# Routing of a mixture of experts inside attention: new segments, capped steps, masks and counts made otherwise

## The chip, the cores and the metric

One Trainium2 chip, one of its cores. The metric is the device time of one execution in microseconds. Below, PE is TensorE, DVE VectorE, ACT ScalarE, POOL GpSimd, and SP the engine that issues most transfers.

## The reference, cut to what matters

Local attention with a few global columns (4 batches, 8 heads, 768 positions, head size 64) makes x, 3072 rows of 512. Then each row goes to two of eight experts:

```python
logits = x @ w_gate
noisy = logits + log1p(exp(x @ w_noise)) * noise
top2 = argpartition(-noisy, 2)[:, :2]; top2_w = softmax of the two
for e in range(8):                       # F = 1024, D = 512
    h = maximum(x[mask] @ w1[e], 0)
    out[mask] += top2_w * (h @ w2[e])
```

## The kernel before

The 3072 rows are 24 blocks of 128 tokens (six to a batch). **Attention** is a loop of 48 rounds, numbered 0 to 47, two to a block; a round takes four heads. Its work is software-pipelined: `score(n+2)` (DVE adds the bias and takes the maximum, ACT exponentiates), `trans` (PE), `product(n+4)` (PE, into the two banks that `score` has just read), `norm(n-4)` (DVE), `attend(n-2)` (PE). Block g is gated in rounds 2g+4 and 2g+5: `gate_t` (transposes, and a copy by POOL that is stored to `xd`), `gate_l` and `gate_s` (logits, made for two blocks at once, and alone for the last block of a segment of odd length).

**Routing** (`route`) is a generator for each segment of consecutive blocks. Its steps: softplus of the noise logits by a polynomial; the two best experts of a token (MAX8 and index, a block each); weights (`weigh`); one-hot counts summed over tokens by PE (lines 530 to 534), which with `carry`, the count of all segments before, give every token its slot in its expert's list; then for each block and choice a mask of the slot's low seven bits (`mask`, line 559, into `wall`, 5 buffers) and a product of value and band (`marks`, line 587), which PE multiplies (line 612) and DVE adds to `tab` (line 615). So segments must pass the counts in order. Steps are dealt out to rounds: `tick(place)` issues one step at each of seven places of a round (0 to 3 in `score`, 4 to 6 in `norm`), `finish()` up to 5 (3 for segments 0 and 1) at its end. A step that yields True goes on at place 4 of the next round, one that yields LAST at place 6, one that yields 2 at `finish`. Segment CLOSE = 2 goes first.

When CLOSE is done, expert 0's first 512 slots are complete enough to use: four `gather`s (POOL's indirect transfers, one a round), then four `whole_words` (16 copies by POOL), then `turn` (PE transposes, ACT and DVE) and **up(0)**: 96 matmuls of 512 columns, with 32 slots between them. The two last segments, `late` (index 3) and `last` (index 4), are advanced in these slots to step numbers that a table gives (`slots`); `split` makes expert 0's second weights. After up(0) DVE does the other six `split`s, the last `tab`, and `rank()`, which orders the experts by count; after it POOL gathers the tokens of expert 0's tail and of expert 1, and weights of ranked experts are fetched. The experts run to the end one after another.

```python
SEG = [(0, 6), (6, 12), (12, 17), (17, 21), (21, NT)]
gather(0, t, DUMP + z * P); yield LAST       # t = 0..3, after CLOSE's last tab
for t in range(TA): whole_words(0, t); yield
for x in pending: x.upto(99)                 # after up(0) and the splits
rank()
```

## Time and profile before

| what | value |
|---|---|
| median of 3 runs (range) | 710.76 us (708.8 to 712.78) |
| the profiled execution, its span | 717.22 us, 715.4 us |
| PE busy, weight loads | 690.2 us (96%), 617.7 us (86%) |
| DVE, ACT, POOL busy | 469.7 us (66%), 425.0 us (59%), 330.0 us (46%) |
| granted PE clock | 0.997 |

Busy time of PE has modelled ends, so a round's length is read from the starts of its matmuls. Attention's last round ends at about 161 us, up(0) runs from 165.77 to 192.42 us, `rank()` ends at about 202.5 us.

### The profile page before, as it was taken

The page shows a single profiled execution, that of the slowest core. Times are in us where ns is not written, and L with a number is a line of the kernel's source. Part 1 is how long each engine was busy: PE and PEld are TensorE (multiplying, and loading weights), DVE is VectorE, ACT ScalarE, POOL GpSimd, SP SyncE. Part 2 cuts the span into 40 slices and gives each one's busy share as a digit, 9 for nine tenths or more (in the row PEclk, how much of TensorE's full clock was granted, in tenths as well). Part 3 has the DMA queues.
Part 4 walks back from the last instruction along what each step waited for, and adds up shares of the span by engine and source line. Part 5 has one row for each costly group of instructions (what it writes and reads, how often), then busy time and mean ns, then how long its engine had stood idle before and what let it go on. Part 6 is the DMA issues. An engine that isn't in the chain of part 4 may idle for free.

```text
span 715.4 us, 16240 instructions
## 1 busy us (share of the span) xinstructions
PE 690.2 (96%) x5769; PEld 617.7 (86%) x5769; DVE 469.7 (66%) x1478; ACT 425.0 (59%) x909; POOL 330.0 (46%) x424
## 2 busy tenths in 40 slices
PE   6999999999999989999999999999999999999995
PEld 5888888877789879999989998999899899889984
DVE  6659898967957557736774686567576766666600
ACT  6888777763427477545854676476558556745510
POOL 3363626372078862074607461644465344642222
PEclk9999999999999999999999999999999999999998
DMA  9997678775086795156935681768459646943233
GB/s 246 317 288 229 205 235 278 229 272 216 0 219 152 130 205 153 16 94 154 184 83 112 169 210 49 135 162 176 76 127 196 128 117 159 204 74 89 31 45 47
DMA packets 129913, 111.10 MB, mean 155 GB/s; under 512 B 51578, under 2 KB 96762, under 8 KB 129824
## 3 DMA queue, kind: packets, MB, share of 16 engines
q1 hardware_dynamic: 118416, 83.84, 43.4%
q0 software_dynamic: 11264, 25.89, 19.8%
q8 instruction: 47, 0.77, 0.5%
q10 hardware_dynamic: 144, 0.26, 0.2%
q14 instruction: 42, 0.34, 0.2%
HBM read 71.07 MB, written 27.59 MB: 138 GB/s over the span
## 4 chain that ended last, share of the span: by engine, by line
PE 67%; DVE 10%; issue 8%; DMA 5%; ACT 4%; POOL 4%; SPq 0%; POOLq 0%; ACTq 0%; DVEq 0%
PE bank L1410 24%; PE av L1148 20%; PE av L878 5%; PE sc L827 4%; PE at L857 4%; PE av L1171 4%; DMA xt<-xg 2%; PE at L1111 2%; DVE xl L196 1%; PE sc L1111 1%; DMA xg<-xd,ids 1%; POOL out_dram L1124 1%; DVE ns L841 1%; PE m L397 1%; ACT xg L277 1%
## 5 line engine op out<-in xcount | busy, mean ns | idle before, releaser
L1410 PE MATMUL bank<-xh,wall 128*128 128x384 f32 (+4 forms) x784 | 216.8, 343 | 3.9 <-ACT aside L1451 3.9
L1410 PEld LDWEIGHTS bank<-xh,wall 128*128 128x128 f32 x784 | 143.8, 188 | 8.3 <-ACT aside L1451 4.7
L1410 PE MATMUL bank<-xl,wall 128*128 128x384 f32 (+4 forms) x392 | 133.3, 340 | 0.0
L1148 PE MATMUL av<-w2h,hh 128*128 128x512 f32 x304 | 119.8, 394 | 2.0 <-ACT aside L1180 1.4
L1124 POOL DMA_INDIRECT out_dram<-y,ids x40 | 63.6, 1590 | 125.6 <-ACT y L1121 121.3
L1148 PE MATMUL av<-w2h,hl 128*128 128x512 f32 x304 | 119.1, 392 | 0.0
L1148 PE MATMUL av<-w2l,hh 128*128 128x512 f32 x304 | 119.0, 391 | 0.0
L196 DVE TENSOR_TENSOR wall<-raw,wall 128x512 fp32r<-128x512 f32 (+1 forms) x84 | 77.7, 931 | 56.0 <-ACT wall L195 55.9
L195 ACT ACTIVATE wall<-raw 128x512 fp32r<-128x512 f32 (+1 forms) x84 | 58.0, 698 | 45.7 <-POOL raw L1256 45.6
L1096 DVE SCALAR_TENSOR_TENSOR hl<-bank,hh 128x384 fp32r<-128x384 f32 (+4 forms) x84 | 47.2, 562 | 55.0 <-ACT hh L1092 52.7
L844 ACT ACTIVATE a<-ns,mx 128x168 f32<-128x168 f32 (+1 forms) x192 | 67.9, 423 | 20.1 <-DVE mx L841 19.4
L243 POOL DMA_INDIRECT xg<-xd,ids x53 | 56.2, 1060 | 45.4 <-DVE place L297 32.5
L1410 PEld LDWEIGHTS bank<-xl,wall 128*128 128x128 f32 x392 | 73.9, 188 | 2.8
L1148 PEld LDWEIGHTS av<-w2h,hl 128*128 128x128 f32 x304 | 57.1, 188 | 12.6
L1148 PEld LDWEIGHTS av<-w2h,hh 128*128 128x128 f32 x304 | 57.2, 188 | 11.6 <-ACT aside L1180 1.7
L1148 PEld LDWEIGHTS av<-w2l,hh 128*128 128x128 f32 x304 | 57.1, 188 | 9.3 <-DVE w2l L196 0.3
L841 DVE CUSTOM_DVE_ANT_0 ns<-sc,bias 128x168 f32<-128x168 f32 (+1 forms) x188 | 51.8, 320 | 19.1 <-PE sc L827 14.1
L1092 ACT ACTIVATE hh<-bank 128x384 fp32r<-128x384 f32 (+4 forms) x84 | 41.8, 498 | 37.5 <-DVE bank L1483 24.0
L1255 POOL TENSOR_TENSOR raw<-raw 128x256 f32<-128x256 f32 x28 | 22.1, 791 | 82.1 <-DVE wall L196 81.4
L235 POOL COPY xt<-y 128x256 uint16<-128x256 uint16 x96 | 35.2, 403 | 51.5 <-DVE y L894 51.5
L878 PE MATMUL av<-vs,at 128*64 128x65 f32 (+1 forms) x768 | 57.3, 224 | 0.0
L878 PEld LDWEIGHTS av<-vs,at 128*64 128x64 f32 (+1 forms) x768 | 50.9, 136 | 2.4 <-issue 2.0
(219 smaller groups left out, 1494.8 us busy)
## 6 DMA issues: line engine op xcount, KB each, us to landing
raw<-in_w SPq DMA_DIRECT2D x64, 256.0 KB
raw<-in_w SPq DMA_DIRECT2D x32, 512.0 KB
out_dram<-zero SPq DMA_DIRECT2D x14, 512.0 KB
vs<-in_v SPq DMA_DIRECT2D x24, 260.0 KB
xd<-xt SPq DMA_DIRECT2D x24, 256.0 KB
qbuf<-in_q SPq DMA_DIRECT2D x23, 256.0 KB
ks<-in_k SPq DMA_DIRECT2D x20, 272.0 KB
vp<-in_v SPq DMA_DIRECT2D x20, 195.0 KB
```

The lines of the kernel that those rows point to most:

```text
L195: nc.scalar.activation(hi, src, AF.Copy)
L196: eng.tensor_sub(lo, src, hi.bitcast(F32))
L235: nc.gpsimd.tensor_copy(to[:, :, c], frm[:, :, c])
L243: nc.gpsimd.indirect_dma_start(out=xg[e, t].bitcast(U16)[:m], out_offset=None, in_=xd[:n], in_offset=bass.IndirectOffsetOnAxis(ap=r, axis= ...
L841: nc.vector.tensor_tensor_reduce(out=ns[x][:, s, :w], in0=ps[:, s], in1=bias[:, u + x, s] if i else bias0[:, u + x, s], scale=-scale, scal ...
L844: nc.scalar.activation(A[n + x][:, s * w:(s + 1) * w], ns[x][:, s, :w], AF.Exp, bias=mx[x][:, s:s + 1], scale=-1.0)
L878: nc.tensor.matmul(ps[s * Q:(s + 1) * Q, h], a[r:z, part * P + q0:part * P + q0 + Q], t[r:z, c], start=k == 0 and (n == 1 or h == 0), stop ...
L1092: nc.scalar.activation(inner(e)[0][j][:, f, :src.shape[1]], src, AF.Relu)
L1096: nc.vector.scalar_tensor_tensor(lo, src, 0.0, hi.bitcast(F32), op0=OP.max, op1=OP.subtract)
L1124: ins = nc.gpsimd.indirect_dma_start(out=out, out_offset=bass.IndirectOffsetOnAxis(ap=r, axis=0), in_=y, in_offset=None, bounds_check=N + ...
L1148: nc.tensor.matmul(ps, x[j][:, f, cols], w[:, f], start=n == 0, stop=n == 3 * FC - 1)
L1410: nc.tensor.matmul(ps, wb[c % 2][u][:, 2 * a + k], x[v][:, 2 * b + k], start=start and n == 0, stop=stop and n == 5, skip_group_check=True)
```

## The change

Segments become 6, 4, 6, 4, 4 blocks, all even, so every block is gated in a pair; CLOSE ends at block 15 instead of 16, so it starts two rounds earlier, and the gathers of expert 0 draw on 16 blocks. Each round may issue at most 5, 5, 9 and 4 steps of segments 0 to 3, and 7 of segments 0 and 1 together. The counts are one matmul of all blocks by `upper` and w by `ones`, each shifted by one block. The two `marks` of a block are one operation of twice the size. Masks are kept in 12 buffers; those of segments 0, 1 and 3 are made by POOL, some rounds or slots ahead, those of CLOSE and of the last segment by DVE (before: 0, 1 and CLOSE by POOL, the others by DVE). Each segment has one group of matmuls at line 612 instead of groups of three blocks. The slots of up(0) are dealt anew.

```diff
--- before.py
+++ after.py
@@ -63,7 +63,7 @@
     windowed = 1 <= n_local <= NP + 1 and 0 <= n_global <= NG
     scale = 1.0 / math.sqrt(D)
     slopes = [2.0 ** (-8.0 * (h + 1) / H) for h in range(H)]
-    SEG = [(0, 6), (6, 12), (12, 17), (17, 21), (21, NT)]
+    SEG = [(0, 6), (6, 10), (10, 16), (16, 20), (20, NT)]
     CLOSE = 2
     SW = max(z - a for a, z in SEG)
 
@@ -524,14 +524,13 @@
         else:
             yield 2
         ps = lgp
-        pos = ps[:, E:(w + 1) * E].rearrange("p (t e) -> p t e", t=w)
-        tot = ps[:, :E]
-        for i in range(w):
-            nc.tensor.matmul(pos[:, i], upper, ohs[:, i], start=True, stop=i == 0)
-            for j in range(i):
-                nc.tensor.matmul(pos[:, i], ones, ohs[:, j], start=False, stop=j == i - 1)
-        for j in range(w):
-            nc.tensor.matmul(tot, ones, ohs[:, j], start=j == 0, stop=j == w - 1)
+        pos = ps[:, :w * E].rearrange("p (t e) -> p t e", t=w)
+        tot = ps[:, w * E:(w + 1) * E]
+        of = ohs.rearrange("p t e -> p (t e)")
+        nc.tensor.matmul(ps[:, :w * E], upper, of, start=True, stop=False, skip_group_check=True)
+        for d in range(1, w + 1):
+            nc.tensor.matmul(ps[:, d * E:(w + 1) * E], ones, of[:, :(w + 1 - d) * E], start=False, stop=d == w,
+                             skip_group_check=True)
         if r != CLOSE:
             yield from some(4)
         else:
@@ -554,10 +553,10 @@
         put_in = {}
 
         def mask(i):
-            m = wts.tile([P, 2, P], FR, name="m", bufs=5)
+            m = wts.tile([P, 2, P], FR, name="m", bufs=12)
             for j in range(2):
-                (nc.vector if r > CLOSE else nc.gpsimd).tensor_scalar(m[:, j], iota_p, row[:, i, j:j + 1], None,
-                                                                      op0=OP.is_equal)
+                (nc.vector if r in (CLOSE, len(SEG) - 1) else nc.gpsimd).tensor_scalar(m[:, j], iota_p, row[:, i, j:j + 1], None,
+                    op0=OP.is_equal)
             put_in[i] = m
 
         nc.vector.tensor_copy(si, sl)
@@ -565,10 +564,6 @@
         nc.vector.tensor_scalar(si, si, P - 1, None, op0=OP.bitwise_and)
         yield
         nc.vector.tensor_copy(row, si)
-        if r == CLOSE and not marking:
-            marking.append(r)
-            for i in range(w):
-                mask(i)
         yield
         nc.vector.tensor_sub(fs, sl, row)
         yield
@@ -576,41 +571,44 @@
         nc.vector.tensor_tensor(band, fs[:, :, :, None].to_broadcast(bs),
                                 first[:, None, None, :].to_broadcast(bs), op=OP.is_equal)
         yield
-        size = w if r == CLOSE else 3
+        size = w
         groups = [range(i, min(i + size, w)) for i in range(0, w, size)]
         def marks(i):
             b = gp.tile([P, Dm], F32, name="xg", bufs=7)
             c = b[:, :6 * E * TT].bitcast(FR).rearrange("p (j x t) -> p j x t", j=2, t=TT)
-            cs = [P, 3 * E, TT]
-            for j in range(2):
-                what = ev[:, i, j].rearrange("p x e -> p (x e)")[:, :, None]
-                nc.vector.tensor_tensor(c[:, j], what.to_broadcast(cs),
-                                        band[:, i, j][:, None, :].to_broadcast(cs), op=OP.mult)
+            cs = [P, 2, 3 * E, TT]
+            what = ev[:, i].rearrange("p j x e -> p j (x e)")[:, :, :, None]
+            nc.vector.tensor_tensor(c, what.to_broadcast(cs), band[:, i][:, :, None, :].to_broadcast(cs), op=OP.mult)
             put_in[i] = put_in[i], c
 
-        while r <= CLOSE and marking and marking != [r]:
-            yield True
-        if r not in marking:
-            marking.append(r)
+        if r <= CLOSE:
+            for i in range(w):
+                mask(i)
+                yield True if r < CLOSE and i % 2 else None
+            while marking:
+                yield True
+        elif r < len(SEG) - 1:
+            for i in range(w):
+                mask(i)
+            yield
+        marking.append(r)
         for x, gr in enumerate(groups):
-            if r <= CLOSE and not put_in:
-                for i in gr:
-                    mask(i)
             for i in gr:
-                if r > CLOSE:
-                    mask(i)
-                marks(i)
-                if r == CLOSE:
-                    yield 2 if i == w - 1 else True if i == 1 else None
+                if r <= CLOSE:
+                    marks(i)
+                    yield 2 if i == w - 1 else True if i % 2 else None
                 else:
-                    yield from (None, ) if r < CLOSE else (None, ) * 3
-            if r != CLOSE:
-                yield from (True, 2) if r < CLOSE else (None, ) * 3
+                    if i not in put_in:
+                        mask(i)
+                    marks(i)
+                    yield from (None, ) * 3
+            if r > CLOSE:
+                yield from (None, ) * 3
             ps = lgp[:, (SW + 1) * E:][:, :3 * E * TT]
             m = [(m[:, j], c[:, j]) for i in gr for m, c in [put_in.pop(i)] for j in range(2)]
             for k, (l, o) in enumerate(m):
                 nc.tensor.matmul(ps, l, o, start=k == 0, stop=k == len(m) - 1)
-            yield LAST if r == CLOSE else True
+            yield LAST if r <= CLOSE else True
             yield
             nc.vector.tensor_add(tab, tab, ps.rearrange("p (x e t) -> p x e t", x=3, e=E))
             yield
@@ -775,12 +773,21 @@
 
         END, WAIT = 7, 8
 
+        PACE = {0: 5, 1: 5, 2: 9, 3: 4, 'all': 7}
+        left = {}
+
         def begin():
+            left.update(PACE)
             for x, _ in active:
                 x.ready = {WAIT: 4, WAIT + 1: 6}.get(x.ready, 0)
 
+        def may(r):
+            return left[r] > 0 and (r >= CLOSE or left['all'] > 0)
+
         def go(y):
             x = y[0]
+            for r in (y[1], 'all') if y[1] < CLOSE else (y[1], ):
+                left[r] -= 1
             v = next(x, 0)
             if v == 0:
                 active.remove(y)
@@ -793,13 +800,13 @@
 
         def tick(place):
             for y in sorted(active, key=lambda y: y[1] != CLOSE):
-                if y[0].ready <= place:
+                if y[0].ready <= place and may(y[1]):
                     return go(y)
 
         def finish():
             for y in active[:]:
                 n = 5 if y[1] >= CLOSE else 3
-                while n and y in active and y[0].ready <= END:
+                while n and y in active and y[0].ready <= END and may(y[1]):
                     go(y)
                     n -= 1
 
@@ -1197,13 +1204,13 @@
         late, last = pending
         slots = {
             0: [(late, 24)], 1: [gate_t, (late, 27)], 2: [(late, 30)], 3: [gate_l, (late, 33)],
-            4: [(late, 36)], 5: [gate_s, (late, 39)], 6: [(late, 42)], 7: [(late, 45), (last, 2)],
-            8: [], 9: [(late, 48), (last, 5)], 10: [(last, 7)], 11: [(last, 8)],
-            12: [(late, 52), (last, 9)], 13: [(last, 12)], 14: [(last, 14)], 15: [(late, 54), (last, 16)],
-            16: [(last, 19)], 17: [(last, 21)], 18: [(last, 23)], 19: [(last, 26)],
-            20: [(last, 30)], 21: [(last, 33)], 22: [(late, 57), (last, 35)], 23: [(last, 37)],
-            24: [(last, 39)], 25: [(last, 42)], 26: [(late, 61)], 27: [(last, 45)],
-            28: [(last, 48)], 29: [(late, 99), split], 30: [split], 31: [(last, 52)],
+            4: [(late, 37)], 5: [gate_s, (late, 40)], 6: [(late, 43)], 7: [(late, 46), (last, 2)],
+            8: [(last, 4)], 9: [(late, 49), (last, 6)], 10: [(last, 8)], 11: [(last, 10)],
+            12: [(late, 52), (last, 12)], 13: [(last, 14)], 14: [(last, 16)], 15: [(late, 55), (last, 18)],
+            16: [(last, 20)], 17: [(last, 23)], 18: [(last, 25)], 19: [(last, 27)],
+            20: [(late, 57)], 21: [(last, 29)], 22: [(late, 99)], 23: [(last, 33)],
+            24: [(last, 36)], 25: [(last, 39)], 26: [(last, 42)], 27: [(last, 45)],
+            28: [(last, 48)], 29: [(last, 51), split], 30: [split, (last, 54)], 31: [(last, 55)],
         }
         slot, parts = [0], [0]
 
```

## Rows read from the trace of the kernel before

**Rows 1.** Windows view; four rounds a row, last up(0): window, length, busy (instructions), PEclk, DMA.
```profile
32.88:44.52 11.64, 11.64 (x250) 10.12 (x243) 6.95 (x44) 10.26 (x29) 6.08 (x8) 1.00 1.05 334
...
56.42:70.72 14.30, 13.70 (x280) 11.69 (x273) 13.10 (x89) 11.51 (x32) 5.39 (x15) 1.00 0.69 203
70.72:82.93 12.21, 12.21 (x256) 10.82 (x249) 10.36 (x63) 9.78 (x28) 8.84 (x18) 1.00 0.70 204
...
94.90:108.16 13.26, 13.17 (x279) 11.50 (x272) 12.13 (x87) 10.44 (x30) 3.06 (x9) 1.00 0.79 231
...
120.38:132.95 12.57, 12.25 (x212) 9.96 (x207) 11.69 (x86) 8.88 (x28) 4.47 (x11) 1.00 1.00 310
132.95:149.04 16.09, 15.28 (x284) 13.08 (x278) 13.29 (x78) 10.96 (x31) 10.75 (x20) 1.00 0.45 137
...
165.77:192.42 26.65, 26.39 (x147) 20.92 (x148) 23.36 (x124) 7.23 (x16) 0.28 (x1) 1.00 0.30 109
```
**Rows 2.** Timeline of TensorE: the counts of segment 0, and the start of up(0).
```profile
68.19 0.20 PE L530 MATMUL lg<-aside,upper 128*128 128x8 bf16 x2
...
68.88 0.31 PE L857 MATMUL at<-ident,a 128*128 128x128 f32 x1
...
163.61 1.47 PE L342 MATMUL sc<-ident,xg 128*128 128x128 f32 x8 [0.49 <-POOL xg L235]
...
165.77 0.50 PE L1111 MATMUL at<-wall,xh 128*128 128x512 f32 x1 [0.54 <-ACT wall L344]
```
**Rows 3.** Chain that ended last, 136 to 167 us: start us, us, what.
```profile
139.89 4.50 POOL wall L559 x7
...
150.64 0.40 issue
...
151.43 0.35 issue
```
**Rows 4.** Timeline of GpSimd at the end of attention.
```profile
155.22 1.03 POOL L243 DMA_INDIRECT xg<-xd,ids  x1
156.25 1.65 POOL L235 COPY xg<-xg 128x256 uint16<-128x256 uint16 x4
...
159.97 4.73 POOL L235 COPY xg<-xg 128x256 uint16<-128x256 uint16 x12
```
**Rows 5.** Timeline of VectorE: small routing operations, then the end of up(0) and after.
```profile
130.43 0.15 DVE L483 MAX8 aside<-aside 128x8 f32<-128x8 f32 x1
...
130.64 0.15 DVE L483 MAX8 aside<-aside 128x8 f32<-128x8 f32 x1
...
177.97 0.18 DVE L462 TENSOR_TENSOR aside<-aside 128x24 f32<-128x24 f32 x1
178.19 0.18 DVE L464 TENSOR_TENSOR aside<-aside 128x24 f32<-128x24 f32 x1
...
188.94 0.48 DVE L559 TENSOR_SCALAR wall<-iota_p,aside 128x128 fp32r<-128x128 f32 x2
189.33 0.57 DVE L587 TENSOR_TENSOR xg<-aside 128x168 fp32r<-128x168 f32 x2
189.82 0.69 DVE L1096 SCALAR_TENSOR_TENSOR hl<-at,hh 128x512 fp32r<-128x512 f32 x1
...
192.74 0.69 DVE L1096 SCALAR_TENSOR_TENSOR hl<-sc,hh 128x512 fp32r<-128x512 f32 x1
...
196.95 0.33 DVE L615 TENSOR_TENSOR tab<-tab,lg 128x168 f32<-128x168 f32 x1
```
**Rows 6.** Operations of lines 587, 559 and 307: count, duration min/median/max ns, first and last start.
```profile
L587 DVE TENSOR_TENSOR xg<-aside x48: 316/327/500, 75.5 to 191.1; 128x168 fp32r<-128x168 f32 x48
...
L559 POOL TENSOR_SCALAR wall<-iota_p,aside x34: 594/636/882, 74.9 to 143.8; 128x128 fp32r<-128x128 f32 x34
L559 DVE TENSOR_SCALAR wall<-iota_p,aside x14: 278/281/286, 173.0 to 190.6; 128x128 fp32r<-128x128 f32 x14
...
L307 DVE TENSOR_TENSOR xg<-perm,tab x2: 808/809/810, 199.2 to 200.5; 128x343 f32<-128x343 f32 x2
```

## The prediction

> **What bounds the kernel now.** I read the busy times first: PE is the engine that is nearly always occupied, so a change in routing can pay only where it takes work or waiting off PE's path. Second, the windows view, cut at the first `attend` matmul of every fourth round, tells where routing costs time. Four rounds without routing take 11.64 us, all of it PE [rows 1]; that is my floor. The reader is to see that length follows VectorE's load: 6.95 us of DVE at the floor, 10.36 in a window of 12.21 us, 12.13 in 13.26, 13.10 in 14.30, 13.29 in 16.09 [rows 1]. The reason is in the code: `product(n+4)` writes the banks that `score(n+2)` reads, and each of score's four operations has a routing step behind it in DVE's queue.
>
> Not all above the floor is waiting; some is PE's own routing work. The counts of a six-block segment, 27 matmuls, hold PE from 68.19 to 68.88 us [rows 2], 0.69 us or 0.0256 each. The 0.57 us over the floor in the window from 70.72, where DVE does not press, I take as one group of six matmuls of line 612, 0.095 each. What is left is stall: rounds 17 to 20, 14.30-11.64-0.69 = 2.0; 29 to 32, 13.26-11.64-0.69 = 0.9; 37 to 40, 12.57-11.64-0.57 = 0.4; 41 to 44 with CLOSE's 20 counts (0.5) and 10 matmuls (0.95), 16.09-11.64-1.45 = 3.0. Together 6.3 us. That is the most the new pacing can save.
>
> Third, the chain of waits says what ends the last of these: CLOSE's masks on POOL, seven of them 4.50 us in the chain [rows 3], PE standing behind them at line 612. A little later two pauses of 0.40 and 0.35 us have no releaser ("issue") between matmuls of `gate_l` [rows 3]; transfers are dense then, and nothing in the change aims at them.
>
> Fourth, the transition. POOL's copies for `whole_words` end at 159.97+4.73 = 164.70 us [rows 4], PE waits 0.49 us for them in `turn` and up(0) starts at 165.77, 1.07 us behind them [rows 2]. Last, DVE's timeline at the end of up(0): it runs without a gap from `hl` at 189.82 to `tab` at 196.95 [rows 5], and `rank` waits for that, the gathers for `rank`. From there the steps are as before, so a shift of `rank` is passed on to the end.
>
> **The change part by part.** I followed the yields by hand through the rounds for both versions; the counts of steps are from that.
>
> *Counts.* In attention 27+27+20 = 74 matmuls become 7+5+7 = 19. The old ones cost 74 x 0.0256 = 1.9 us. The new ones have up to 48 columns, which no row shows for these operands: at least 0.0256 each (0.5 us), at most the 0.095 of a 168-column one (1.8 us). The weights are the same and 48 is nearer 8 than 168: I take 0.035, 0.7 us. Gain 1.2 (0.1 to 1.4). Line 612 has 32 matmuls there instead of 34: 0.2. In up(0), 23 counts become 10 (-0.24) and 14 of line 612 become 16 (+0.19): nothing.
>
> *Merged products.* Two operations of 168 elements start 0.245 us apart (189.33 to 189.82 for two) [rows 5], 327 ns long [rows 6]. One of 336 is bounded by rows: not under the 0.245 of one, and not over the 0.81 us that line 307 takes for 343 elements [rows 6]. Twice 0.245 less one start-up is 0.42, my value, since the inner strides are those of line 587 and not those of the transposed table of line 307. So 0.07 us a block gained, and 0.3 lost at the upper end. The Trainium skill (VectorE: DVE Perf Modes, section on the TRN2 errata) gives N+151 cycles of 0.96 GHz for such an operation in fp32, that is 332 ns at 168, which the trace agrees with, and 515 ns at 343, where line 307 measured 809. By it a merged product lasts 507 ns and saves 0.16 us a block, 24 blocks 3.8 us of DVE, most of it where DVE has room.
>
> *Masks.* Two on DVE take 0.39 us (188.94 to 189.33) [rows 5], on POOL 0.64 each [rows 6]. CLOSE's 12 go to DVE: 2.3 us more there, and POOL's wait is gone. Segments 0 and 1 keep POOL, now two rounds or more ahead of use. Segment 3's eight leave DVE: 1.6 us less in up(0).
>
> *Pacing.* Segment 0 now spreads from round 15 to 31, segment 1 from 23 to 38, CLOSE from 35 to 44. In rounds 17 to 20 at most 5 steps a round remain of up to 10 and the window falls under the 10.4 us of DVE that ran free. The load does not vanish: rounds 37 to 40 get CLOSE's searches (six at 0.21, 130.43 to 130.64), seven polynomial steps and some 21 small operations (0.21 back to back, 177.97 to 178.19 [rows 5]; I take half, an estimate, since score's operations stand between them and cover their latency), three products by `ohj` (0.45), four blocks' masks (1.6) and segment 1's last two products (0.8). With the small ones at 0.10, 1.3+0.7+2.1+0.45+1.6+0.8 = 6.9 us over the 6.95 of the floor. So 13.9 us of DVE, as loaded as the worst window of before; by the rows at 12.13 and 13.10 (0.9 and 2.0 of stall) I put 2.5 there. Rounds 25 to 28 (both segments, four searches, two products) 0.5, 41 to 44 0.5: stall 3.5 in place of 6.3, gain 2.8. Bounds: 0 and 6.3.
>
> *CLOSE and the gathers.* CLOSE starts two rounds earlier (35, not 37), but with nine steps a round, six blocks and a pause after each second product its last `tab` and first gather come in round 44, before in round 43. So the fourth gather comes in round 47, where `whole_words` of the first tile stood, and all 16 copies follow instead of 12. Behind them in POOL's queue stand only the last block's copies. The gather (1.03 us) takes the place of the four copies that filled POOL's gap at 156.25 [rows 4]; 16 copies at 4.73/12 = 0.394 are 6.31 us, 1.58 more from the same start. PE waited there already, so I add 1.6 to the start of up(0). Bounds: 0, if attention's end moves, and 2.
>
> *Slots.* `last` reaches its matmuls at slot 31 as before, `late` ends seven slots earlier. But `last` has a fourth block: behind `hl` at 189.82 DVE now has two blocks' masks and products, 2 x 0.81 = 1.6, where one (0.88) and a `tab` (0.24) stood. DVE has no gap there, so `rank` comes 0.5 later (0 to 1.8, the latter at line 307's price).
>
> *Even segments.* As many `gate_l` matmuls, one pair less alone: nothing, hidden in PE's ACT waits; uncovered some 0.1. Expert 0's list from 16 blocks holds 509 rows in the data (worked out from the reference), three slots empty; 724 of its 812 are used, so no overflow path.
>
> Sum: -1.4 (counts, line 612) -2.8 (stall) +1.6 (transition) +0.5 (tail) = -2.1 us. Against the profiled execution's 717.22 us that is 715.1; the same difference from the median of 710.76 gives 708.7 us. The profiled execution was 6.5 us above the median, but the differences are of stages that every execution has.
>
> **The rivals.** *The caps do all they could.* If DVE's queue is short enough in every round, stall falls to 1 (-5.3), counts cost their lower bound (-1.6), and the two fetch-like pauses (0.75, and as much again in PE's restart, an estimate) are not met again because PE's stream is shorter: -1.5. With +1.6 and nothing in the tail -6.8: 704.0. For it: windows with DVE at 10.4 ran free. Against: CLOSE's rounds stay full.
>
> *The merged product is dear (slower).* At line 307's 0.81 us, 0.74 from start to start, each costs 0.32 more than I took. Ten lie in rounds 36 to 44 where DVE is full (3.2), six in half-full rounds (some 1.0), four in the tail (1.3): 5.5 on -2.1 makes +3.4, and with the 612 group waiting for the last of them some +4: 714.8. It decides from about 0.8 us an operation. Against it: line 587's own strides.
>
> *POOL's masks hold DVE up.* In up(0) eight of POOL's masks now lie beside DVE's products and subtractions. If each held DVE for its 0.64 us and none met a gap, +5.1: 713.8. Against it: line 587 has a median of 327 ns and a minimum of 316 [rows 6], though some of its 48 ran while POOL made masks. The Trainium skill (SBUF — State Buffer, section "Who interferes with whom") has the rule: a DVE operation with two SBUF inputs and a POOL operation that reads SBUF share a port, and the second to issue fully blocks. By that rule these products would show gaps of up to a mask; the trace does not show them in the median, only in a maximum of 500 ns.
>
> **How the numbers follow.** About 0.5% (3.6 us) is what can be told from no change. My sum 0.50, with an own range of 706 to 711.5; the first rival 0.34; dear products 0.08; POOL's masks 0.04; else 0.04, evenly. Faster by over 0.5% (under 707.2): 0.34 and a share of the sum's lower end, 0.38. Slower (over 714.3): 0.11. Within: 0.51. The range reaches from the first rival's side to the dear products: 703.5 to 714.5.
>
> **What would show it.** Right: the four-round window after segment 0's start near 12.3 us, the stretch of rounds 37 to 40 the longest (over 14 us), no wait of line 612 for POOL; fourth gather directly before the last block's copies, PE waiting some 2 us in `turn`; `tab` some 5 us behind the last matmul of up(0). Line 587 at 0.45 to 0.55 us. Wrong: line 587 at 0.8; rounds 37 to 40 at 12.5 us (the first rival); or a shift between `rank` and the first expert's weights, which I took as rigid.

## The result, and the profile after

The changed kernel took 720.53 us (median of 20 executions, 709.34 to 724.37), the kernel before beside it 712.52 us (20 executions, 708.80 to 716.99). The ratio is 1.0059, 95% interval 1.003 to 1.0087: slower by about 0.6%. The forecast was 708.7 us, between no change and a small gain, and the measured time lies above its range of 703.5 to 714.5. Medians, here and below, are over all executions, while a ratio and its interval leave out those more than 1.5% above the fastest of their kernel (11 of the 20 of the changed kernel, and one of 953 us in experiment 3 and one of 957 us in experiment 5, both at a mean clock of 0.656), so that ratios and medians do not divide into each other. The profiled execution took 718.29 us with a span of 716.5 us.

First the windows view of the changed kernel: the same rounds as in [rows 1], two windows after CLOSE's masks and two around the turns. The columns are those of [rows 1]; the third from the end is the granted clock, 1.00 being 2.4 GHz and 0.50 being 1.2 GHz.

```profile
33.52:45.16 11.64, 11.64 (x251) 10.13 (x244) 6.95 (x44) 10.25 (x29) 6.10 (x8) 1.00 1.09 342
57.04:69.65 12.61, 12.50 (x253) 10.83 (x246) 10.66 (x80) 11.06 (x31) 4.81 (x14) 1.00 0.70 218
69.65:81.40 11.75, 11.75 (x256) 10.46 (x248) 9.74 (x66) 9.86 (x30) 3.79 (x10) 1.00 0.86 246
92.61:106.67 14.06, 13.63 (x269) 12.27 (x262) 10.90 (x67) 9.86 (x29) 2.97 (x8) 1.00 0.83 249
118.26:132.70 14.44, 13.12 (x234) 10.70 (x227) 14.23 (x104) 9.52 (x28) 3.81 (x8) 1.00 0.95 313
132.70:151.32 18.62, 16.99 (x263) 14.96 (x256) 13.55 (x73) 11.31 (x31) 2.97 (x8) 0.82 0.76 227
136.00:140.00 4.00, 3.15 (x47) 2.98 (x46) 2.91 (x17) 2.96 (x9) 0.74 (x2) 0.59 0.68 236
140.00:144.00 4.00, 4.00 (x46) 3.46 (x42) 1.48 (x6) 1.76 (x4) 0.74 (x2) 0.56 0.88 244
164.00:168.00 4.00, 0.19 (x1) 0.22 (x2) 3.97 (x7) 0.21 (x1) 3.12 (x9) 0.93 0.00 0
168.00:172.00 4.00, 3.31 (x12) 2.62 (x12) 2.44 (x10) 1.19 (x2) 0.00 (x0) 0.50 0.84 307
```

The floor of 11.64 us is the same. Rounds 17 to 24 gained (14.30 and 12.21 us became 12.61 and 11.75), and rounds 37 to 40 grew to 14.44 us as forecast. Rounds 29 to 32 grew from 13.26 to 14.06 us, TensorE busy for 13.63 of them, since segment 0's twelve matmuls of line 610 now fall there. Rounds 41 to 44, forecast as nearly free of stall, grew from 16.09 to 18.62 us. The reader should then look at the clock: in [rows 1] it is 1.00 everywhere, here it is near half in two places, behind two waits of TensorE. What these waits are, the chain of waits of the changed kernel says (start us, us, what).

```profile
132.96 0.68 DVE wall L558 x3
...
133.84 0.67 DVE wall L558 x3
134.51 0.24 DVE ns L848
...
134.76 0.40 DVE wall L558 x2
135.15 0.24 DVE ns L848
...
135.40 0.40 DVE wall L558 x2
135.79 0.24 DVE ns L848
...
136.86 0.95 PE sc L834 x9
...
148.16 1.51 PE lg L610 x12
...
163.00 3.40 DVE ixf L491
...
167.07 0.61 DVE wall L345
...
167.81 1.95 PE sc L342 x8
```

The first: CLOSE's twelve masks (line 558, now on VectorE) stand in front of and between score's operations (L848), so that the next product (L834) starts only at 136.86. The second: a conversion of 128 x 8 indices (line 491) holds VectorE for 3.40 us, and the turns' subtraction (L345), for which TensorE's next transposes (L342) wait, is queued behind it. VectorE's timeline shows the conversion and the reciprocal behind it, and a merged product at the end of up(0):

```profile
162.60 0.40 DVE L489 TENSOR_TENSOR aside<-aside 128x4 f32<-128x4 f32 x1
162.93 3.48 DVE L491 CAST ixf<-aside 128x8 f32<-128x8 uint32 x1
163.31 3.10 DVE L898 RECIPROCAL den<-den 128x4 f32<-128x4 f32 x1
...
196.80 0.50 DVE L581 TENSOR_TENSOR xg<-aside 128x336 fp32r<-128x336 f32 x1
197.22 0.47 DVE L558 TENSOR_SCALAR wall<-iota_p,aside 128x128 fp32r<-128x128 f32 x2
...
203.44 0.32 DVE L613 TENSOR_TENSOR tab<-tab,lg 128x168 f32<-128x168 f32 x1
...
205.60 0.47 DVE L303 CAST who<-cnt 1x7 int32<-1x7 f32 x1
```

GpSimd's timeline over the same stretch: eighteen copies without a pause, ending at 165.63 + 0.74 = 166.37 us; the conversion ends at 162.93 + 3.48 = 166.41.

```profile
159.47 6.25 POOL L235 COPY xg<-xg 128x256 uint16<-128x256 uint16 x16
165.63 0.74 POOL L235 COPY xt<-y 128x256 uint16<-128x256 uint16 x2
```

TensorE's timeline from there. The product of 512 columns of up(0) starts every 0.43 us at half clock (171.45 to 171.88).

```profile
167.81 1.94 PE L342 MATMUL sc<-ident,xg 128*128 128x128 f32 x8 [4.46 <-DVE wall L345]
170.44 0.79 PE L1118 MATMUL at<-wall,xh 128*128 128x512 f32 x1 [0.69 <-ACT wall L344]
...
171.45 0.63 PE L1118 MATMUL at<-wall,xh 128*128 128x512 f32 x1
171.88 0.63 PE L1118 MATMUL at<-wall,xl 128*128 128x512 f32 x1
```

In the kernel before, the operation of `rank` that writes `who` stands here:

```profile
199.13 0.38 DVE L303 CAST who<-cnt 1x7 int32<-1x7 f32 x1
```

Up to it the two profiles differ by 6.47 us: 0.81 to the last matmul of `attend`, 3.86 from there to the first of up(0), 1.80 from there to `who`, which takes 33.36 us before and 35.16 after. Of the 0.81 us, 0.65 stand already at the first round, so that the 48 rounds together took 0.16 us more: what some gained, others lost.

### The profile page after: what moved, and what is told of

Same layout as the page of the kernel before. It is cut to its first block, busy times and chain, and to the rows that moved or that the text cites. A ratio compares the mean times of both kernels' runs of the same rounds, so it can differ in the third digit from the quotient of the medians.

```text
span 716.5 us, 16069 instructions
## 1 busy us (share of the span) xinstructions
PE 690.0 (96%) x5699; PEld 620.4 (87%) x5699; DVE 465.9 (65%) x1457; ACT 425.5 (59%) x908; POOL 324.1 (45%) x418
## 4 chain that ended last, share of the span: by engine, by line
PE 73%; DVE 9%; issue 7%; DMA 5%; POOL 3%; ACT 3%; SPq 0%; POOLq 0%; ACTq 0%; DVEq 0%
PE bank L1417 24%; PE av L1155 20%; PE av L885 6%; PE av L1178 5%; PE sc L834 4%; PE at L864 4%; DMA xt<-xg 2%; PE at L1118 2%; PE sc L1118 2%; POOL out_dram L1131 1%; DVE ns L848 1%; PE m L375 1%; DVE xl L196 1%; DMA xg<-xd,ids 1%; PE m L397 1%
## 5 line engine op out<-in xcount | busy, mean ns | idle before, releaser
L848 DVE CUSTOM_DVE_ANT_0 ns<-sc,bias 128x168 f32<-128x168 f32 (+1 forms) x188 | 53.6, 319 | 21.6 <-PE sc L834 16.2
```

The source lines that it names most:

```text
L848: nc.vector.tensor_tensor_reduce(out=ns[x][:, s, :w], in0=ps[:, s], in1=bias[:, u + x, s] if i else bias0[:, u + x, s], scale=-scale, scal ...
```

## The experiments

In the diffs, NORMS stands for the loop over the two last norms ahead of the turns. The expectations count the rounds from the first `attend`: their 39 and 40 are the prediction's 41 and 42. A table of the times on which the reading rests stands behind the experiments.

**1. CLOSE's masks back on GpSimd (in the changed kernel).**

```
-  (nc.vector if r in (CLOSE, len(SEG) - 1) else nc.gpsimd).tensor_scalar(m[:, j], ...
+  (nc.vector if r == len(SEG) - 1 else nc.gpsimd).tensor_scalar(m[:, j], ...
```

> The changed kernel with one edit: CLOSE's twelve masks go back to GpSimd. Theory A (VectorE's queue in round 40, eight masks between the operations of one score, stops TensorE, and the stop is what lowers its clock for the next 6.8 us): rounds 39 to 42 take about 3.3 us each instead of 4.8 and 6.1, the granted clock stays at full speed through attention, one low stretch is left (before up(0)), the time falls by 3 to 5 us against the changed kernel, to about that of before. Rival B (the clock falls by itself, in any kernel of this length, wherever): two low stretches as often as with the change, the time within 1.5 us of the changed kernel. Rival C (GpSimd's masks are too slow for line 610): TensorE waits there for GpSimd again, 1 us or more.

714.05 us, ratio to before 1.000 (0.9959 to 1.0041). The windows view of this kernel for rounds 41 to 44:

```profile
130.90:144.32 13.42, 13.42 (x262) 12.13 (x255) 11.11 (x62) 10.73 (x31) 9.55 (x19) 1.00 0.70 207
```

TensorE is busy throughout. 13.42 us instead of 18.62, and no wait for GpSimd's masks: in the changed kernel's order of steps they are made early enough. The transition is as in the changed kernel, with its conversion of 3.48 us and a stretch of half clock behind it.

**2. No routing steps in the two last norms (in the changed kernel).** The steps that stood there, line 491 among them, are issued behind the turns.

```
+ kept_back, active[:] = active[:], []
  for n in NPAIR - 4, NPAIR - 2:
-     begin()
      norm(n)
+ active[:] = kept_back
+ begin()
+ left[3] = 9
```

> The changed kernel with one edit: the two last norms issue no routing step, the same steps are issued behind the four turns (as they fell in the kernel before). Theory A (the conversion of the expert numbers, line 491, which reads and writes SBUF alone, cannot start while GpSimd copies without a gap, and the turns' subtractions stand behind it): line 491 back at 0.17 us instead of 3.5, TensorE waits about 2 us instead of 4.5 before the last turns, up(0) starts some 2.5 us earlier, no low clock there, rank 4 to 6 us earlier. Rival C (it is GpSimd's longer row of copies alone, 16 instead of 12): up(0) starts at most 1 us earlier and the clock still falls. Rival B (the clock falls by itself): low stretches as often as before the edit.

716.57 us, ratio 1.0016 (0.9975 to 1.0058). The conversion takes at most 175 ns, TensorE waits 1.07 us ahead of the last turns instead of 4.46, up(0) starts 4.54 us behind the first turn instead of 8.18, and from there to `rank` it takes 33.40 us. The masks still stall rounds 41 to 44, with the clock at 1.00 this time, so that their price without it can be read from the windows view, 15.59 - 13.42 = 2.17 us:

```profile
131.34:146.93 15.59, 13.96 (x262) 12.34 (x255) 13.39 (x73) 10.97 (x31) 2.97 (x8) 1.00 0.83 253
```

This execution lost time elsewhere: TensorE waited 7.20 us for the first expert's tokens, which ScalarE (line 277) got late from a transfer.

```profile
257.67 1.34 ACT L277 ACTIVATE xg<-xt 128x1024 uint16<-128x1024 uint16 x1 [7.99 <-DMA xt<-xg]
```

**3. Both edits.**

> Both edits. Theory A: no low stretch before the end, and the time is 6 to 9 us under the changed kernel, that is 2 to 4 us under the kernel before, since the gains of the first two segments' pacing and of the counts are left. Rival B: still two low stretches in most runs, within 2 us of the changed kernel.

710.46 us, ratio 0.9975 (0.9936 to 1.0014), an interval that lies below the changed kernel's. By the medians it is 10.1 us below the changed kernel, and the two edits alone give 6.5 and 4.0; by the ratios it is 6.0, 4.2 and 3.1. So the two about add up, within the intervals. Theory A's clock did not come true: the profile keeps one stretch at a low clock behind the turns, and another (0.58 from 262 to 266) at the wait for the first expert's tokens.

```profile
160.00:164.00 4.00, 3.68 (x11) 2.97 (x12) 3.50 (x28) 0.47 (x2) 0.59 (x2) 0.57 0.65 236
```

**4. One conversion ahead of the turns (in the kernel before).**

```
  NORMS
+ nc.vector.tensor_copy(probe[1], probe[0])      # 128 x 8, uint32 to float32
```

> The kernel before with one operation added: a conversion of 128x8 unsigned numbers to f32 on VectorE, behind the last norm, ahead of the four turns, that nothing reads (its source is set to zero at the start). Theory A: it lasts until GpSimd's copies end, some 2 to 3.5 us instead of 0.17, up(0) starts 1 to 2 us later, and where TensorE stands still so long its clock falls in the stretch after. The time rises by 2 to 5 us. Rival C (the operation in the changed kernel was slow for another reason, as a late input): 0.2 us here, the time as before within 1 us.

711.88 us, ratio 1.0001 (0.9968 to 1.0035). The conversion, of eight numbers in a row, took 0.45 us, not 2 to 3.5: it waited for one copy of GpSimd and no more. That a conversion beside GpSimd's copies always waits them out was wrong.

```profile
160.89 0.45 DVE L1054 CAST probe<-probe 128x8 f32<-128x8 uint32 x1
```

**5. CLOSE's masks on VectorE (in the kernel before).**

```
-  (nc.vector if r > CLOSE else nc.gpsimd).tensor_scalar(m[:, j], ...
+  (nc.vector if r >= CLOSE else nc.gpsimd).tensor_scalar(m[:, j], ...
```

> The kernel before with one thing of the change alone: the eight masks of CLOSE's four blocks by VectorE. Theory A (these masks, some 0.26 us each as line 558 took in the changed kernel, stand among score's and attend's operations on VectorE and stop TensorE): a wait of TensorE of 1 us or more ahead of a product appears in the two rounds behind the masks, which grow by 1.5 to 3 us together; in return the wait for GpSimd's 4.50 us of masks goes, so that the time stays within 2 us of before. A stretch of the granted clock below 0.7 behind that wait would bear out that the clock's fall comes with TensorE's pauses. Rival B (the stall of rounds 39 and 40 in the changed kernel came from the new order of steps, in which the marks of four blocks fall into the same rounds, and not from the masks' engine): the two rounds stay within 0.5 us of what the kernel before shows, and the time falls by 1 to 3 us, because the wait for GpSimd goes for nothing.

720.65 us, ratio 1.0101 (1.0053 to 1.0148), four executions. (The segment has five blocks here, ten masks, not the eight that the expectation says.) VectorE's and TensorE's timelines show the masks in one piece and the product behind them 2.38 us late ("issue", since the operation it waits for is not named):

```profile
137.54 2.12 DVE L559 TENSOR_SCALAR wall<-iota_p,aside 128x128 fp32r<-128x128 f32 x10
```
```profile
141.71 1.20 PE L827 MATMUL sc<-ks,qbuf 64*64 64x168 f32 x13 [2.38 <-issue]
```

That round takes 6.06 us where it took 3.92, the next 4.02 where it took 5.20 with its wait for GpSimd [rows 3]: +1.0 for the pair, less than theory A's 1.5 to 3, because part of the wait for GpSimd went in return. So theory A holds for the place, the masks' engine alone makes a stall of 2.14 us in one round, and the new order of steps isn't needed for it. Theory A's time, within 2 us of before, was wrong: the whole time rose by much more. `rank` is only 0.44 us later than in the profile before, and the rest stands in the waits for the first expert's tokens (2.37 and 5.06 us against 1.40 and 2.48 before), with a low clock behind. Whether these belong to the edit, four executions don't settle.

**6. A pause of TensorE (in the kernel before).**

```
  NORMS
+ for j in range(6):
+     nc.vector.tensor_add(idle, idle, idle)     # 128 x 512
```

> The kernel before with six additions of 128 x 512 float32 on VectorE, some 0.6 us each, put behind the last norm and ahead of the turns, where the changed kernel's conversion stood for 3.48 us; their result is used nowhere. Theory (a pause of TensorE of about 4 us there is followed by a stretch of half the clock, as in the changed kernel): the wait ahead of the last turns is 4 to 5 us instead of 1, the first product of the experts starts some 3.6 us later, a stretch of 3 to 10 us at a granted clock of about 0.5 to 0.6 stands behind it, and from there to the first operation of the rank it takes 34.5 to 36 us instead of 33.4; the time grows by 5 to 6 us. Rival (the clock's fall belongs to something else in the changed kernel): the clock stays at 1.00 behind the pause, the 33.4 us stay, and the time grows by 3 to 4 us. Second rival (what is late here is made good downstream): the time grows by less than 2 us.

723.65 us, ratio 1.011 (1.0052 to 1.0167). The wait was 5.32 us, and the windows view shows half the clock behind it, which the kernel before doesn't have there:

```profile
164.00:168.00 4.00, 0.15 (x1) 0.18 (x2) 3.90 (x6) 0.00 (x0) 4.00 (x7) 0.87 0.00 0
168.00:172.00 4.00, 3.58 (x14) 3.16 (x15) 2.53 (x16) 1.20 (x2) 0.05 (x1) 0.50 0.79 295
172.00:176.00 4.00, 4.00 (x32) 2.85 (x34) 2.43 (x18) 0.80 (x2) 0.00 (x0) 0.78 1.03 378
```

From up(0) to `rank` it takes 34.86 us instead of 33.36. The theory's price was too low (5 to 6 us): in the profile the start of up(0) is 4.7 us later, the stretch up to `rank` is 1.5 longer, and a wait of 5.50 us for the first expert's tokens stands further on.

**7. Six conversions of two shapes (in the kernel before).** Four stand between the two last norms, two behind them; the strided ones are line 1056, the others line 1054.

```
+ def cast(j, even):
+     if even: nc.vector.tensor_copy(flat[j], probe[:, 0])
+     else:    nc.vector.tensor_copy(flat[j] as 4 x 2, probe[:, :, :2])
```

> The kernel before with three conversions of the changed kernel's very shape (128 x 4 x 2 float32 from the first two of every eight uint32) and three of eight uint32 in a row, put behind the two last norms, in the stretch in which GpSimd copies its twelve tiles; their results are used nowhere. Theory A (any conversion waits for a gap in GpSimd's copies, so how long is chance of the place): some of the six take over 1 us, of both shapes. Theory B (only the strided shape waits): the three strided ones take 1 us or more each, the others at most 0.5. Theory C (no such wait; the 3.48 us in the changed kernel were something else): all take 0.5 us or less.

VectorE's timeline, of which the other four repeat the two:

```profile
160.54 0.44 DVE L1056 CAST flat<-probe 128x8 f32<-128x8 uint32 x1
160.84 0.16 DVE L1054 CAST flat<-probe 128x8 f32<-128x8 uint32 x1
```

One execution, 717.01 us. The strided ones take 0.44 to 0.46 us, to the end of the copy that runs, the others 0.16. None waits out the row of copies: theory C's bound held, and A's and B's fell. The strided shape alone didn't make 3.48 us. That the shape decides whether a conversion waits for one copy isn't shown either: each of the short ones stood directly behind a strided one that had just waited, and the conversion of experiment 4, eight in a row too, took 0.45 us.

**8. Line 491 by another operation (in the changed kernel).**

```
- nc.vector.tensor_copy(ixf, ix[:, :, :2])
+ nc.vector.tensor_tensor(ixf, ix[:, :, :2], ix[:, :, :2], op=OP.max)
```

> The changed kernel with one operation written otherwise: the conversion of the indices (line 491) as a maximum of the indices with themselves by two-operand tensor operation, with the same result. Theory A (the copy-like conversion is what stood 3.48 us behind GpSimd's copies; a two-operand operation does not wait, as the turns' subtractions of 0.64 us beside the same copies do not): line 491 takes 0.3 us or less, the wait of TensorE ahead of the last turns falls from 4.46 us to about 1, the first product of the experts starts 3 to 3.6 us earlier, and the time falls by 3 to 5 us against the changed kernel, to about the second experiment's 716.6. Rival B (any operation there waits, whatever its kind, because it reads what GpSimd holds): line 491 keeps 3 us or more and the time stays at 720.

```profile
162.52 0.47 DVE L491 TENSOR_TENSOR ixf<-aside 128x8 f32<-128x8 uint32 x1
162.90 0.17 DVE L898 RECIPROCAL den<-den 128x4 f32<-128x4 f32 x1
```

In the same place, beside the same row of sixteen copies, 0.47 us instead of 3.48, and the reciprocal 0.17 instead of 3.10. TensorE waits 1.94 us, up(0) starts 5.28 us behind the first turn instead of 8.18. 717.99 us, ratio 1.0035 (0.9987 to 1.0083): by the medians 2.5 us below the changed kernel, less than theory A said and not clear of noise, since the intervals overlap. The stretch of half clock behind the turns is still there (0.70 and 0.50 in the windows from 164 to 172).

**9. Experiment 6, its pause filled.**

```
  if t == 2:
      gate_l(NT - 2)
+     for _ in range(20): nc.tensor.matmul(idle_ps, ident, ident, start=True, stop=True)
  turn(0, t, bank("sc"))
```

> The sixth experiment (the kernel before with six additions on VectorE ahead of the turns) with one thing more: twenty products of the 128 x 128 identity with itself on TensorE, ahead of the third turn, into a bank that nobody reads before it is overwritten. TensorE then works while it would wait 5.32 us for VectorE. Theory (the clock falls behind a pause of TensorE): the wait ahead of the third turn is 0 to 1.5 us, the first product of the experts starts within 0.5 us of where the sixth experiment has it, the granted clock stays at 1.00 from there on instead of 0.50 to 0.78 over 168 to 176, and from the first product to the rank it takes 33.4 us; the time falls by 3 to 6 us against the sixth experiment's 723.65. Rival (the clock falls for some other reason, such as VectorE's additions): the stretch of half clock stays and the time is within 2 us of the sixth experiment's.

718.12 us, ratio 1.0041 (1.001 to 1.0071), by the medians 5.5 us below experiment 6, whose interval (1.0052 to 1.0167, four executions) this one overlaps. TensorE's timeline (two records for each product) and the windows view:

```profile
163.25 4.73 PE L1058 MATMUL at<-ident 128*128 128x128 f32 x40
168.68 1.23 PE L342 MATMUL sc<-ident,xg 128*128 128x128 f32 x8 [0.71 <-DVE wall L345]
...
170.60 0.50 PE L1122 MATMUL at<-wall,xh 128*128 128x512 f32 x1 [0.54 <-ACT wall L344]
```
```profile
164.00:168.00 4.00, 3.98 (x36) 3.79 (x34) 3.86 (x6) 0.00 (x0) 4.00 (x6) 1.00 0.01 4
168.00:172.00 4.00, 2.77 (x16) 2.30 (x17) 3.16 (x15) 1.20 (x2) 0.89 (x3) 1.00 0.58 216
```

up(0) starts where it did (170.60 against 170.48; from the first turn 8.95 us instead of 9.61), and yet the clock stays at 1.00, and from up(0) to `rank` it takes 33.34 us. The mean clock of all ten executions is 0.995 to 0.999, of experiment 6's four 0.982 to 0.990. So it is TensorE's standing still after which the clock fell here, VectorE's additions being the same, and useless products keep it up.

**10. The conversion a little later (in the changed kernel).** One unused subtraction of 128 x 4 is put ahead of line 491 of the fourth segment.

> The changed kernel with one subtraction of 128 x 4 more on VectorE, unused, just ahead of the conversion at line 491 of the fourth segment, which starts some 0.08 to 0.15 us later by it. Theory A (the conversion stood 3.48 us because of its moment: in the changed kernel and in the first experiment it began 0.02 us ahead of the start of a GpSimd copy, whereas the probes, which took 0.44 to 0.46 us, began 0.04 to 0.07 us behind one): it takes 0.5 us or less now, and the first product of the experts comes some 3 us earlier. Theory B (it is the conversion with its place in memory and its neighbours, at any moment): it takes 3 us or more again.

The conversion took 3.1 us, TensorE waited 4.51 us, 720.30 us (ratio 1.0045, 0.9987 to 1.0102). But the moment was not moved: the subtraction itself waited for a copy, and the conversion began again just ahead of the next. So the two theories stay undecided, and the hold-up is shown to repeat.

**11. The changed kernel, its second wait filled** (as in experiment 9, with 17 products, and 2 ahead of up(0)).

> The changed kernel with seventeen products of the identity with itself on TensorE ahead of the third turn and two ahead of the first product of the experts, into a bank that nobody reads. The wait of 4.46 us for VectorE is then filled, and nothing is made earlier. Theory (the second stretch of half clock in the changed kernel comes from this wait and costs what the stretch loses): the wait is below 1.5 us, no window from 164 to 180 is below 0.9, from the first product to the rank it takes 33.4 us instead of 35.2, and the time falls by 1 to 3 us against the changed kernel; the stretch at 136 to 144 stays. Rival: the stretch stays, or goes without the time falling, since the clock falls elsewhere in its place.

717.60 us, ratio 1.0054 (1.0018 to 1.0091): by the medians 2.9 us below the changed kernel, by the ratios no different from it. In the profiled execution the conversion took only 0.50 us, so that there was little to fill; it can't say what the fill did. Over the ten executions the mean clock (median) is 0.994 instead of 0.9875. This execution also shows the masks' stall (4.52 and 3.32 us for the two rounds) with the clock at 1.00.

**12. Experiment 3 with its waits filled** (4 and 2 products).

> The third experiment (masks of CLOSE back on GpSimd, no steps of the routing in the two last norms) with four idle products of the identity ahead of the third turn and two ahead of the experts' first product, where TensorE waited 1.07 and 0.69 us and a stretch of 3.41 us at about 0.57 of the clock followed. Theory: that stretch goes, from the first product to the rank it takes 33.4 us instead of 34.9, and the time is 1 to 2 us below the third experiment's 710.5, at a ratio of 0.993 to 0.997 to before; runs at a mean clock of 0.998 lie at 705 to 707. Rival (the fill itself delays the turns by as much as the clock gives back, or a wait for the transposed tokens of the next expert takes it up): 710 to 712, ratio 0.997 to 1.000.

710.98 us, ratio 0.9968 (0.9934 to 1.0002). The fill does what it was put in for:

```profile
160.00:164.00 4.00, 3.70 (x25) 2.79 (x24) 3.41 (x23) 1.41 (x4) 1.44 (x5) 1.00 0.43 155
```

up(0) to `rank` is 33.40 us instead of 34.93. But the time is that of experiment 3: 710.98 us is in the rival's range, the ratio at the border of the two. A low clock stands later, at the wait for the first expert's tokens (0.91 in the window from 260 to 280), as it does in experiment 3's profile too; so what became of the 1.5 us isn't shown.

The table: median time, median over the executions of the mean granted clock, and from the profile the length of rounds 41 to 44, the time from the first turn to up(0) and from up(0) to `rank`, all us.

| kernel | time | mean clock | 41 to 44 | turn to up(0) | up(0) to rank |
|---|---|---|---|---|---|
| before (82 executions, beside the experiments) | 712.9 | 0.996 | 16.09 | 4.32 | 33.36 |
| changed | 720.5 | 0.9875 | 18.62 | 8.18 | 35.16 |
| 1 masks on GpSimd | 714.0 | 0.991 | 13.42 | 8.16 | 36.09 |
| 2 no steps in last norms | 716.6 | 0.9915 | 15.59 | 4.54 | 33.40 |
| 3 both | 710.5 | 0.9945 | 13.42 | 4.54 | 34.93 |
| 6 before, pause | 723.7 | 0.9885 | | 9.61 | 34.86 |
| 8 other operation | 718.0 | 0.9935 | 18.61 | 5.28 | 35.81 |
| 9 before, pause filled | 718.1 | 0.998 | | 8.95 | 33.34 |
| 12 both, filled | 711.0 | 0.994 | 13.43 | 4.57 | 33.40 |

## Why the prediction was wrong

Slower by over 0.5% had a chance of 0.11, for dear products and for GpSimd's masks; both fell, and what made the kernel slower had no rival of its own. The sum failed at three steps. Without the masks' stall (experiment 3) rounds 17 to 44 take 89.1 us instead of 92.6, -3.5, where the sum had -2.8 for stall and -1.4 for counts and line 612.

**Pacing, rounds 41 to 44: the step that failed first.** I put four of CLOSE's six blocks of masks into rounds 37 to 40 as 1.6 us of VectorE's time and gave "41 to 44 0.5" of stall. All twelve masks came at the seam of the two, from 132.25 on, eight ahead of one score and two behind each of its first two operations: not as load, but as a block in the queue ahead of what TensorE waits for. Their price is 2.17 us (experiments 2 and 11 against 1 and 3, all at a clock of 1.00). Without them the four rounds take 13.42 us; my own terms, the floor, one count group, twelve matmuls of line 610 and 0.5 of stall, make 11.64 + 0.2 + 1.1 + 0.5 = 13.4. That this meets the 13.42 is luck: TensorE was busy in all of it, without stall, and the twelve matmuls took 1.51 us, 0.126 each where I had 0.095. The wait for GpSimd [rows 3], which moving the masks was to remove, is gone with GpSimd's masks too (experiment 1). Elsewhere 14.44 us for 37 to 40 ("over 14") and 12.61 for 17 to 20 ("near 12.3") are as forecast. Rounds 29 to 32 are not: my terms make 11.64 + 0.2 + 1.1 = 12.9 there, without stall, and they took 14.06, 0.43 of it a wait of the counts for `tab` and 0.4 the dearer matmuls.

**The transition: a term mis-sized by its mechanism.** I took +1.6 us from GpSimd's copies and held that TensorE waits for those. What came last was VectorE: +3.86 us, of which experiment 8 takes back 2.90 by changing one operation, and experiment 2 all but 0.2. In experiment 2 GpSimd's 16 copies follow on each other as I had it, so my term for them, 1.6, comes to no more than 0.2 there. I had looked at what stood behind the fourth gather in GpSimd's queue, but not at what routing step now stood ahead of the turns' subtractions in VectorE's. There the conversion, in the profile before behind the turns, met a row of copies without a pause. The Trainium skill (SBUF — State Buffer, section "Who interferes with whom") has casts among the operations that may take the port pair shared with GpSimd, and lets the later of two block fully. The trace agrees that they block, and is worse in one point: three times a conversion waited not for the running copy but for all that followed, 3.48, 3.48 and 3.1 us. The prediction had weighed this rule for products of two operands alone; a two-operand operation in the conversion's place was held up no longer than one copy (0.47 us in experiment 8). The hold-up does not come in every execution: in experiment 11's, with the same code ahead of it, the conversion took 0.50 us.

**The clock: a term that was not there.** [Rows 1] show 1.00 in every window, so the sum was made at one clock. In the profiled execution both waits were followed by half of it: rounds 41 and 42 took 4.80 and 6.07 us in the changed kernel against 4.52 and 3.32 in experiment 11 with the same masks (3.03 us), and up(0) to `rank` took 1.8 us more. Experiments 6 and 9 show the cause: the same pause, idle or filled, 34.86 or 33.34 us behind it, with mean clocks that do not overlap. The Trainium skill (TensorE: Matmul & The Clock Gate, section "Part 1: The HAM clock gate") says that the gate follows how busy the engine has lately been; experiments 6 and 9 agree. Not every pause is followed by it: the masks' stall was not in experiments 2 and 11 (1.00 in rounds 41 to 44), nor the waits of 1.40 and 2.48 us of the kernel before. Over all executions the median of the mean clock is 0.9875 against 0.996, which at 717 us is at most some 6 us of lost clock (an estimate) out of the medians' difference of 8; the profiled execution shows 3.03 + 1.80. The one execution of the changed kernel at 0.998 took 709.34 us. That this lies near the forecast of 708.7 doesn't bear the sum out: it is one execution without a profile, and the sum had neither the masks' stall nor the conversion in it.

**What held.** The operation behind a merged product starts 0.42 us after it (196.80 to 197.22), the value of the sum, and the product has a median of 499 ns in line 581's rows; the rival that it is dear fell. The Trainium skill (VectorE: DVE Perf Modes, section on the TRN2 errata), from which the prediction worked out 507 ns, was right here. From `hl` to `tab` the tail takes 7.63 us instead of 7.13, the +0.5 of the sum, but it was made good in up(0): 33.40 against 33.36 us to `rank` (experiment 2). GpSimd's masks beside VectorE's products in up(0) cost each of them 0.1 us at most: the products there took 0.50 to 0.60 us, and the longest of all, 703 ns, stands in attention.

```profile
L581 DVE TENSOR_TENSOR xg<-aside x24: 470/499/703, 91.6 to 197.6; 128x336 fp32r<-128x336 f32 x24
```

The "issue" pauses of [rows 3] were not met again in the profile after (that round took 2.62 us instead of 4.90), as the first rival had it, and by more than its 1.5 us; that TensorE's shorter stream is the reason isn't shown. Experiments 3 and 12, without the masks' stall and the conversion, show what is left of the change: their executions at a clock of 0.998 took 706.1 to 709.7 us, those of the kernel before at 0.998 took 708.8 to 714.2.

**The rigid shift.** It is not rigid in one pair of profiles: `rank` is 6.47 us later, the span only 1.1 us longer. TensorE waits 2.9 us less around the first expert's tokens (0.41 and 1.99 us), and about 2 us less from 350 to 380. The kernel before waited for the tokens for 1.40 and 2.48 us besides 1.42 ahead of them:

```profile
258.09 0.45 PE L1410 MATMUL bank<-xh,wall 128*128 128x406 f32 x1 [1.40 <-ACT aside L1451]
268.63 0.45 PE L1410 MATMUL bank<-xh,wall 128*128 128x406 f32 x1 [2.48 <-ACT aside L1451]
```

Against experiment 4, which is the kernel before but for 0.45 us of VectorE, `rank` is 8.31 us later and the span 7.3 longer. That wait differs from execution to execution (1.5 to 8.6 us together in these profiles, behind the transfers that gather and transpose the tokens), so how much of a shift ahead of it is passed on can't be read from one pair.

**What stays open.** Why a conversion was passed over by a whole row of copies in experiments 1 and 10 and in the changed kernel, but not in 4, 7 and 11. By the single records of the trace, in the three it began 0.02 to 0.03 us ahead of a copy, in the others with one or up to 0.07 behind; a two-operand operation began 0.02 ahead and got in (experiment 8). In the three, the operation just ahead of the conversion had itself waited for a copy (0.39 to 0.46 us), in experiment 11 it had not (0.17). Experiment 10 was to part the moment from the place and did not. What makes the transfers in front of the first expert take 12 to 16 us was not tried either.

## What to carry to other kernels

When work is moved to an engine, look at what is queued behind it there at that moment, operation by operation: an engine with room in a window of four rounds can still stop the path for 2 us in one of them. When steps are moved earlier, follow them past every queue, the one of VectorE as well as GpSimd's, and try a two-operand operation in place of a conversion that stands beside a long row of GpSimd copies (experiment 8). A pause of TensorE can cost more than its length, where the clock falls behind it (experiment 6), which not every pause brings (experiments 2 and 11). Useless products in the pause kept the clock up (experiment 9); in experiment 12 they did so too, and no gain in time showed.

## What the runs showed of the hardware that was not expected

A VectorE conversion of 128 x 8, 0.16 us long by itself, stood 3.48 us beside nine GpSimd copies, one every 6.25 / 16 = 0.39 us, until GpSimd had none left; the operation behind it stood until then too (3.10 us). A maximum of two operands in its place took 0.47 us. In other executions a conversion in such a row waited for one copy only (0.44 to 0.50 us). With twenty products of the identity, 4.73 us of TensorE, in a pause, the clock stayed at 1.00 where it had fallen to 0.50, and the stretch behind was 1.5 us shorter.
